# An explicit order for the attention stage, a wait for GpSimd's steps, twelve staged weight tiles and early fill matmuls

## The chip, the cores and the metric

The kernel runs on one core of one Trainium2 chip. The metric is the device time of one execution in microseconds (us). PE is TensorE, DVE VectorE, ACT ScalarE, POOL GpSimd, and SP the queue from which nearly all DMAs are issued. PE's clock has two levels here, 1.2 and 2.4 GHz; the profile gives the granted clock as a share of the higher one.

## What is computed

```python
# attention: q, k, v, a_re, a_im are (4, 8, 768, 48)
mag = np.sqrt(a_re * a_re + a_im * a_im)
scale = np.minimum(mag, 0.999) / (mag + 1e-06)
for t in range(S):
    S = (a_re * scale + i * a_im * scale)[t, :, None] * S + outer(k[t], v[t])   # complex S
    y[t] = q[t] @ real(S)
x = y.transpose(0, 2, 1, 3).reshape(3072, 384)
# first MLP: 8 experts, 384 -> 1024 -> 384, for tokens with x @ w_skip > 0
e_idx = argmax(x @ w_gate); gate = softmax(x @ w_gate)[e_idx]
x = x + gate * (relu(x @ w1[e_idx]) @ w2[e_idx])
# second MLP, all tokens: 384 -> 2048 -> 384
out = relu(x @ w_in) ** 2 @ w_out
```

## The kernel before

Three stages follow each other on the core: attention (to about 284 us), the first MLP, the second MLP.

Attention works on 12 units `u` (4 batches, 3 blocks of 256 positions), each with two chunks of 128 positions. For a unit, `load_a` brings a_re and a_im into two tiles of the pool `ws` (tags of 4 buffers each), `load_qk` brings q and k, `load_v` v. The front of a unit turns a into sums: `ln_r`, `inv_r`, `tangent`, `square`, `ln_s`, `ln_a`, `eps_a`, `fin_l` give the logarithm of the magnitude, `angle` the angle; `total_l` and `total_th` add two halves; `sum_l` and `sum_th` (L1000, L1008) sum them over positions with matmuls into the one PSUM buffer `cs`; `exp_l` and `exp_n` (ACT) give the scales, `whole_turns`, `rest_turns`, `abs_turns`, `cosine` and `sine` the rotations. Logarithm and exponential are one table of ACT, angle, sine and cosine another; going from one to the other issues a table load (L872). `scale_q`, `scale_k` (L1078, L1083), `rot_q`, `rot_k` (L1090, two instructions a unit each) and `shift` (L1105) apply them. For unit 0 the front is split into its two halves.

The core of attention runs over 48 half chunks `kk`: `turn_q`, `turn_k` (four transposes each, L1121), the copies `turned_q`, `turned_k` (L947 on DVE, L945 on ACT), `score` (L1142), `mask` (L1149, DVE), `from_state` (L1164) and `from_chunk` (L1173); and over 24 chunks `j`: `state` (L1184), `state_add`, `state_move`, `state_turn`, `state_turned`, `y_out`, `x_turn`, `x_out`, `x_store` (L1239), and the routing logits `logits`, `logits_out`, `logits_turn`, `logits_sum`. `route` (generators in small pieces) makes the lists of tokens for groups of chunks; after group 2, `gather_a` fetches the first 128 rows of expert 0, and `first_a`, `second_a` compute them at the end of attention.

Every one of these is a job with a queue (P, A, V, G, D for PE, ACT, DVE, POOL, SP), a cost, the jobs that it needs, and the buffers that it takes. `order()` runs a list scheduler over the jobs with due times from the tables `DUE`, `DUE_AT`, `START` and `PHASES`, and the jobs are emitted in the order found; each engine runs its own instructions in that order. `ENG` says which engine takes a copy or an elementwise step. `SHARED` names the steps of DVE that read or write SBUF only; the scheduler lets them and POOL's steps not overlap in its own model, but nothing in the program enforces it.

`load_w(i)` loads tile i of the first MLP's weights into the same pool `ws`. With `WS = 8`, tiles 0 to 7 (expert 0) are loaded in attention; tile 8 + 2g is issued after every second step of `first_rows` of the second half of expert 0's rows, and the second-matmul tiles 9, 11, 13, 15 after steps of `second_rows`. `split_w(i)` casts tile i on ACT (L2134) and takes the rest on DVE (L2135); `NEXT_SPLIT` places tiles 8, 10, 9 in the entry. In the main loop step s issues tile `s + WS`. Ahead of the first MLP `WARM` = 18 fill matmuls are issued (L2264).

## Time and profile before

| | us |
|---|---|
| median of 3 runs | 844.82 (844.55 to 845.34) |
| the profiled execution | 847.55 |
| its span, first to last instruction | 845.8 |
| PE, DVE, ACT, POOL busy | 809.1, 636.5, 402.3, 146.4 |

The profiled execution is 2.73 us longer than the median, and 1.75 us of its time lie outside its span. The busy time of PE is modelled from pipelined matmuls, so a stretch in which PE is shown as busy may still hold fewer matmuls than another; the number of matmuls in a stretch, the idle time before an instruction with its releaser, and the granted clock say more.

### The profile page before, as it was taken

How to read it: one execution, taken by the hardware profiler on the slowest of the kernel's cores; microseconds unless marked ns; L12 is line 12 of the kernel's file. 1: busy time of each engine (PE TensorE's matmuls, PEld its weight loads, DVE VectorE, ACT ScalarE, POOL GpSimd, SP SyncE). 2: the span in 40 equal slices, each digit the busy share in tenths (PEclk: the TensorE clock that was granted, in tenths of full speed). 3: DMA queues.
4: the chain of work that ended last, by engine and by line, in shares of the span. 5: the costliest groups of instructions: out<-in, count | busy, mean ns of one | idle time of the engine just before them, and what ended most of it. 6: DMA issues, size and time to landing. Idle time of an engine off the chain costs nothing.

```text
span 845.8 us, 14533 instructions
## 1 busy us (share of the span) xinstructions
PE 809.1 (96%) x5620; PEld 702.6 (83%) x5620; DVE 636.5 (75%) x1175; ACT 402.3 (48%) x691; POOL 146.4 (17%) x113
## 2 busy tenths in 40 slices
...
GB/s 181 175 181 96 161 122 138 122 103 108 151 146 109 165 297 273 241 241 242 106 107 93 94 112 1 38 0 162 98 83 133 136 175 149 159 141 76 1 1 41
DMA packets 177564, 109.01 MB, mean 129 GB/s; under 512 B 129811, under 2 KB 169001, under 8 KB 177488
## 3 DMA queue, kind: packets, MB, share of 16 engines
...
q0 software_dynamic: 2048, 5.45, 2.2%
q8 instruction: 46, 0.75, 0.4%
...
HBM read 91.52 MB, written 17.30 MB: 129 GB/s over the span
## 4 chain that ended last, share of the span: by engine, by line
PE 81%; DVE 10%; issue 3%; DMA 2%; POOL 1%; ACT 1%; SPq 1%; POOLq 0%; DVEq 0%; ACTq 0%
PE ph L2387 21%; PE po L2416 7%; PE po L2418 7%; PE po L2417 7%; PE ph L2162 7%; PE mp L1142 4%; PE pt L1121 4%; PE cs L1000 3%; PE yp L1173 2%; PE po L2182 2%; PE po L2183 2%; PE po L2184 2%; PE yp L1164 2%; PE up L1184 2%; PE xp L1230 1%
## 5 line engine op out<-in xcount | busy, mean ns | idle before, releaser
L2392 ACT ACTIVATE rl<-ph 128x512 f32<-128x512 f32 x96 | 57.4, 598 | 176.9 <-PE ph L2387 176.9
L2416 PE MATMUL po<-woh,gh 128*128 128x384 f32 x384 | 129.5, 337 | 1.1 <-DVE part L2423 1.1
L2418 PE MATMUL po<-woh,gl 128*128 128x384 f32 x384 | 129.6, 337 | 0.0
L2417 PE MATMUL po<-wol,gh 128*128 128x384 f32 x384 | 129.0, 336 | 0.0
L2394 DVE TENSOR_TENSOR gg<-rl,ph 128x512 f32<-128x512 f32 x96 | 65.9, 686 | 69.6 <-ACT rl L2392 69.6
L2387 PE MATMUL ph<-xh,wih 128*128 128x512 f32 x288 | 114.6, 398 | 0.0
L2387 PE MATMUL ph<-xh,wil 128*128 128x512 f32 x288 | 113.3, 393 | 0.0
L2399 DVE TENSOR_TENSOR gl<-gg,gh 128x512 fp32r<-128x512 f32 x96 | 66.3, 691 | 51.6 <-ACT gh L2397 34.4
L2397 ACT CAST gh<-gg 128x512 fp32r<-128x512 f32 x96 | 59.7, 622 | 88.7 <-DVE gg L2394 88.7
L2387 PE MATMUL ph<-xl,wih 128*128 128x512 f32 x288 | 81.9, 392 | 0.0
L2416 PEld LDWEIGHTS po<-woh,gh 128*128 128x128 f32 x384 | 72.2, 188 | 5.9 <-DVE part L2423 1.7
L2417 PEld LDWEIGHTS po<-wol,gh 128*128 128x128 f32 x384 | 72.1, 188 | 4.0
L2418 PEld LDWEIGHTS po<-woh,gl 128*128 128x128 f32 x384 | 72.0, 188 | 0.0
L2387 PEld LDWEIGHTS ph<-xl,wih 128*128 128x128 f32 x288 | 54.1, 188 | 12.4
L2387 PEld LDWEIGHTS ph<-xh,wih 128*128 128x128 f32 x288 | 53.9, 187 | 8.7 <-ACT xh L2377 0.2
L2387 PEld LDWEIGHTS ph<-xh,wil 128*128 128x128 f32 x288 | 54.2, 188 | 8.2
L1142 PE MATMUL mp<-qhT,khT 96*128 96x128 f32 x384 | 53.6, 285 | 1.4 <-ACT khT L945 1.2
L1090 POOL TENSOR_TENSOR kh<-kn,sc 128x768 f32<-128x768 f32 x22 | 46.1, 2109 | 39.9 <-ACT sc L876 37.6
L1142 PEld LDWEIGHTS mp<-qhT,khT 96*128 96x128 f32 x384 | 46.7, 193 | 6.6 <-issue 3.3
L2162 PE MATMUL ph<-xh,w1h 128*128 128x256 f32 x168 | 44.4, 293 | 2.5 <-DVE hl L2166 2.5
L2165 ACT ACTIVATE hh<-ph 128x256 fp32r<-128x256 f32 x56 | 21.4, 384 | 45.4 <-PE ph L2162 44.8
L2162 PE MATMUL ph<-xh,w1l 128*128 128x256 f32 x168 | 42.3, 280 | 0.0
...
## 6 DMA issues: line engine op xcount, KB each, us to landing
...
```

Of the source, the lines that this page charges most:

```text
L1090: eng("rot_" + n_, u).tensor_mul(x[n_ + "h"][:, c], x[n_ + "n"][:, c].unsqueeze(2).to_broadcast([128, H, 2, D]), scv)
L1121: nc.tensor.transpose(out=pt[0:96, i, :], in_=flat(u[nm], c, h), identity=ident)
L1142: nc.tensor.matmul(out=mp[:, i, :], lhsT=X[kk]["kh"][:, i, :], rhs=X[kk]["qh"][:, i, :], start=True, stop=True)
L2162: mm(out=ph, lhsT=w_[:, c0:c0 + 128], rhs=x_[:, kk], start=(i == 0), stop=(i == len(parts) - 1))
L2387: mm(out=ph, lhsT=w_[:, kk * 128:(kk + 1) * 128], rhs=x_[:, kk], start=(i == 0), stop=(i == len(parts) - 1),)
L2392: nc.scalar.activation(out=rl, in_=ph, func=AF.Relu)
L2394: nc.vector.tensor_mul(gg, rl, ph)
L2397: nc.scalar.copy(out=gh, in_=gg)
L2399: nc.vector.tensor_sub(gl, gg, gh.bitcast(FP32))
L2416: mm(out=po2[j][t], lhsT=a, rhs=wo[f][0], start=begin, stop=False)
L2417: mm(out=po2[j][t], lhsT=a, rhs=wo[f][1], start=False, stop=False)
L2418: mm(out=po2[j][t], lhsT=b_, rhs=wo[f][0], start=False, stop=end)
```

## The change

- The scheduler and its due tables go. `ORDER` is a written list of the 1262 jobs, and `order()` only asserts that each job stands behind what it needs. Which job stands where changes all over attention. In unit 0 the angles and their sums now stand ahead of the rest of the logarithm chain. `load_v` stands in the order of units.
- `ENG` gives many steps to another engine: of 48 each, DVE has 14 `khT` and 15 `qhT` copies (20 and 21 before); `rot_k` is on POOL for 5 units (11 before); `scale_q` and `scale_k` are on POOL for 8 and 6 units (5 and 2 before); `tangent` on POOL for 8 (6 before); `whole_turns` on DVE for 8 (3 before); `x_out` on DVE 6 times (10 before), `y_out` 8 times (12 before).
- The first instruction of each step of POOL (but `gather_a`) waits for the last instruction of the `SHARED` step of DVE that was emitted last before it.
- `WS` is 12: the pool has 6 buffers of each tag, tiles 0 to 11 are loaded in attention, and the later ones are issued at the old places with numbers 4 higher.
- `warm` issues 8 and 6 fill matmuls before attention's own begin, behind `inv_r` and `exp_n` of unit 0. `cst2` is loaded ahead of `cst`.
- `half_hi` and `half_lo` and the tables `HALVES_L`, `HALVES_TH` are added; both are empty, so that no such step is emitted. Costs in the jobs change and no longer have an effect.

```diff
--- before.py
+++ after.py
-DUE = {
...
-}
...
+ORDER = """
+load0.0 load0.1 ln_r.0.0 cst2 cst inv_r.0.0 clear tangent.0.0 square.0.0 ln_r.0.1 inv_r.0.1 tangent.0.1 ln_s.0.0 warm.0
+angle.0.0 square.0.1 angle.0.1 ln_a.0.0 eps_a.0.0 const load_a.1 sum_th.0.0 whole_turns.0.0 sum_th.0.1 rest_turns.0.0 more
+whole_turns.0.1 ln_s.0.1 ln_a.0.1 ln_r.1 fin_l.0.0 eps_a.0.1 inv_r.1 load0k.1 abs_turns.0.0 load_v.0 load0q.0 sum_l.0.0
+exp_n.0.0 exp_l.0.0 fin_l.0.1 rest_turns.0.1 tangent.1 abs_turns.0.1 sum_l.0.1 square.1 exp_n.0.1 scale_k.0.1 warm.1
+load0k.0 sine.0.0 from_state.0 scale_q.0.0 angle.1 scale_k.0.0 total_th.1 sum_th.1.0 cosine.0.0 rot_k.0.0 state.0 load_a.2
+sine.0.1 cosine.0.1 rot_k.0.1 load0q.1 ln_s.1 whole_turns.1.0 rest_turns.1.0 rot_q.0.0 ln_r.2 inv_r.2 load_a.3 turn_k.0
+turned_k.0 ln_a.1 eps_a.1 tangent.2 state_add.0 sum_th.1.1 turn_q.0 exp_l.0.1 turned_q.0 turn_q.1 turned_q.1 whole_turns.1.1
+rest_turns.1.1 turn_k.1 turned_k.1 scale_q.0.1 fin_l.1 total_l.1 score.0 score.1 turn_k.2 turned_k.2 mask.1 turn_k.3
+turned_k.3 abs_turns.1 square.2 ln_s.2 sum_l.1.0 from_state.1 ln_r.3 inv_r.3 load_qk.1 state.1 rot_q.0.1 turn_q.3 exp_n.1.0
...
+first_a.4 logits.23 logits_out.23 first_a.5 logits_turn.23 logits_sum.23 route.4.0 route.4.1 route.3.1000 second_a.0
+second_a.1 route.4.2 route.4.3 route.4.4 first_a.6 route.4.5 route.4.6 route.4.7 route.4.8 first_a.7 relu_a.1 second_a.2
+route.4.9 route.4.10 route.4.1000 second_a.3 second_a.4 x_turn.23 x_out.23 x_store.23 route_exp.4 second_a.5 x_store.22
+second_a.6 second_a.7 yo_a.0
+"""
...
+HALVES_L = ()
+HALVES_TH = ()
...
 ENG = {
-    "abs": "s", "abs@0": "v", "abs@1": "v", "abs@5": "v", "abs@6": "v", "khT": "s", "khT@3": "v", "khT@7": "v",
-    "khT@9": "v", "khT@10": "v", "khT@13": "v", "khT@14": "v", "khT@15": "v", "khT@17": "v", "khT@19": "v",
-    "khT@24": "v", "khT@28": "v", "khT@31": "v", "khT@32": "v", "khT@36": "v", "khT@37": "v", "khT@39": "v",
-    "khT@42": "v", "khT@44": "v", "khT@45": "v", "khT@47": "v", "ls": "s", "ls@0": "v", "ls@1": "v", "ls@2":
-    "v", "ls@4": "v", "ls@6": "v", "ls@7": "v", "ls@13": "v", "ls@15": "v", "ls@23": "v", "qhT": "s", "qhT@4":
-    "v", "qhT@7": "v", "qhT@9": "v", "qhT@10": "v", "qhT@11": "v", "qhT@12": "v", "qhT@14": "v", "qhT@15": "v",
-    "qhT@19": "v", "qhT@21": "v", "qhT@25": "v", "qhT@30": "v", "qhT@31": "v", "qhT@32": "v", "qhT@34": "v",
-    "qhT@35": "v", "qhT@36": "v", "qhT@42": "v", "qhT@43": "v", "qhT@44": "v", "qhT@45": "v", "rot_k": "g",
-    "rot_k@6": "v", "rot_q": "v", "rot_q@4": "g", "rot_q@9": "g", "rot_q@10": "g", "rot_q@11": "g", "scale_k":
-    "v", "scale_k@3": "g", "scale_k@4": "g", "scale_q": "v", "scale_q@0": "g", "scale_q@1": "g", "scale_q@5":
-    "g", "scale_q@6": "g", "scale_q@10": "g", "sd": "s", "sd@0": "v", "sd@1": "v", "sd@6": "v", "sd@7": "v",
-    "sd@10": "v", "sd@12": "v", "sd@14": "v", "sd@16": "v", "shift": "v", "shift@2": "g", "shift@5": "g",
-    "shift@11": "g", "sq": "v", "sq@0": "g", "sq@2": "s", "sq@4": "g", "sq@5": "g", "sq@6": "s", "sq@9": "s",
-    "sq@11": "s", "t": "v", "t@1": "g", "t@3": "g", "t@5": "g", "t@9": "g", "t@10": "g", "t@11": "g", "tot":
-    "g", "tot@1": "v", "tot@5": "v", "tot@7": "v", "whole": "s", "whole@0": "v", "whole@1": "v", "whole@4": "v",
-    "xn": "s", "xn@1": "v", "xn@4": "v", "xn@8": "v", "xn@11": "v", "xn@13": "v", "xn@14": "v", "xn@15": "v",
-    "xn@19": "v", "xn@20": "v", "xn@21": "v", "yT": "v", "yT@2": "s", "yT@3": "s", "yT@4": "s", "yT@7": "s",
-    "yT@8": "s", "yT@9": "s", "yT@12": "s", "yT@15": "s", "yT@18": "s", "yT@19": "s", "yT@20": "s", "yT@21": "s",
+    "abs": "s", "abs@0": "v", "abs@2": "v", "abs@6": "v", "abs@7": "v", "khT": "s", "khT@0": "v", "khT@2": "v",
+    "khT@3": "v", "khT@4": "v", "khT@6": "v", "khT@10": "v", "khT@12": "v", "khT@13": "v", "khT@14": "v",
+    "khT@15": "v", "khT@16": "v", "khT@21": "v", "khT@27": "v", "khT@44": "v", "ls": "s", "ls@3": "v", "ls@5":
+    "v", "ls@8": "v", "ls@13": "v", "ls@15": "v", "ls@17": "v", "ls@20": "v", "qhT": "s", "qhT@0": "v", "qhT@2":
+    "v", "qhT@7": "v", "qhT@10": "v", "qhT@13": "v", "qhT@23": "v", "qhT@26": "v", "qhT@28": "v", "qhT@29": "v",
+    "qhT@34": "v", "qhT@35": "v", "qhT@36": "v", "qhT@42": "v", "qhT@43": "v", "qhT@44": "v", "rot_k": "v",
+    "rot_k@4": "g", "rot_k@7": "g", "rot_k@9": "g", "rot_k@10": "g", "rot_k@11": "g", "rot_q": "v", "rot_q@0":
+    "g", "rot_q@1": "g", "rot_q@3": "g", "rot_q@11": "g", "scale_k": "v", "scale_k@2": "g", "scale_k@3": "g",
+    "scale_k@6": "g", "scale_k@9": "g", "scale_k@10": "g", "scale_k@11": "g", "scale_q": "g", "scale_q@0": "v",
+    "scale_q@5": "v", "scale_q@6": "v", "scale_q@8": "v", "sd": "s", "sd@0": "v", "sd@2": "v", "sd@6": "v",
+    "sd@13": "v", "sd@15": "v", "sd@16": "v", "sd@19": "v", "sd@21": "v", "shift": "v", "shift@4": "g",
+    "shift@7": "g", "shift@11": "g", "sq": "s", "sq@0": "v", "sq@1": "v", "sq@3": "v", "sq@5": "v", "sq@6": "v",
+    "sq@10": "g", "t": "g", "t@0": "v", "t@1": "v", "t@5": "v", "t@7": "v", "tot": "g", "tot@1": "v", "tot@2":
+    "v", "tot@11": "v", "whole": "v", "whole@4": "s", "whole@7": "s", "whole@8": "s", "whole@10": "s", "xn":
+    "s", "xn@0": "v", "xn@7": "v", "xn@8": "v", "xn@15": "v", "xn@18": "v", "xn@19": "v", "yT": "s", "yT@1":
+    "v", "yT@2": "v", "yT@5": "v", "yT@11": "v", "yT@13": "v", "yT@21": "v", "yT@22": "v", "yT@23": "v",
+    "half_hi": "s",
 }
...
 WARM = 18
+WARMS = (8, 6)
+WARM_AFTER = (("inv_r", 0, 0), ("exp_n", 0, 1))
 NEXT_SPLIT = {0: 8, 2: 10, 7: 9}
...
     def clear():
+        nc.gpsimd.memset(made["ones"], 1.0)
         nc.gpsimd.memset(made["ones_t"], 1.0 / TWO_PI)
-        nc.gpsimd.memset(made["ones"], 1.0)
         for t in vt:
             nc.gpsimd.memset(t, 0.0)
         nc.gpsimd.memset(wr, 0.0)
 
     def make_more():
         nc.gpsimd.memset(ones16, 1.0)
+        nc.gpsimd.tensor_copy(out=made["lo_r"], in_=C("lo"))
+        nc.gpsimd.tensor_copy(out=made["hi_r"], in_=made["hi"])
         nc.gpsimd.tensor_sub(strict16, C("lo"), ident)
         nc.gpsimd.tensor_copy(out=iota16, in_=C("iota"))
         nc.gpsimd.memset(run[:, 0, :], 0.0)
+
+    def warm(i):
+
+        if i == 0:
+            spare_bank[0] = ps_u.tile([128, 512], FP32, tag="u", name="warm")
+        for _ in range(WARMS[i]):
+            nc.tensor.matmul(
+                out=spare_bank[0][:, 0:128], lhsT=made["ones"], rhs=made["ones"], start=True, stop=True
+            )
 
...
-    WS = 8
+    WS = 12
...
         D_(("load0", 0), lambda: load0((("ar", a_re), ("ai", a_im)), 0), 2.2, takes=[("ar", fl_), ("ai", ft)])
+        D_(("cst",), lambda: load_const(True), 0.5)
         D_(("load0", 1), lambda: load0((("ar", a_re), ("ai", a_im)), 1), 2.2)
-        D_(("cst",), lambda: load_const(True), 0.5)
-        jobs["load_a", 1]["due"] = -1000 + next(n)
+        for i, after in enumerate(WARM_AFTER):
+            job(("warm", i), warm, (i,), "P", 0.222 * WARMS[i], [("clear",), after], [("u", [("warm", len(WARMS) - 1)])] if i == 0 else [])
         jobs["load_a", 1]["after"] = []
...
-        for key in (("load_v", 0), ("load_a", 2), ("load_qk", 1), ("load_v", 1)):
-            jobs[key]["due"] = -1000 + next(n)
         D_(("wr",), load_wr, 0.5, [("clear",)])
-        job(("clear",), clear, (), "G", 3.3, due=-1000)
-        job(("const",), make_const, (), "V", 0.9, [("cst",)], due=-5.0)
-        job(("more",), make_more, (), "G", 1.6, [("const",), ("cst2",)], due=0.0)
+        job(("clear",), clear, (), "G", 3.3)
+        job(("const",), make_const, (), "V", 0.9, [("cst",)])
+        job(("more",), make_more, (), "G", 2.4, [("const",), ("cst2",)])
         for i in range(WS):
-            job(("load_w", i), load_w, (i,), "D", 2.2, takes=[("ai" if i % 2 else "ar", [])], due=due("load_w", NU, 4, i) + 0.5 * i)
+            job(("load_w", i), load_w, (i,), "D", 2.2, takes=[("ai" if i % 2 else "ar", [])],
+                behind=[("load_w", i - 1) if i else ("load_a", NU - 1)])
         for i in range(3):
-            job(("load_raw", i), load_raw, (i,), "D", 4.4, due=due("load_raw", NU, 4, i) + 2 * i, after=[("load_w", WS - 1)])
+            job(("load_raw", i), load_raw, (i,), "D", 4.4, after=[("load_w", WS - 1)], behind=[("load_raw", i - 1)] * (i > 0))
 
     SIZE = dict(
-        ar=4, ai=4, qn=2, kn=2, r_=4, eL=2, eN=2, totl=1, totth=1, sc=2, qh=2, kh=2, tr_s=2,
...
+    def order():
+
+        by_name = {".".join(map(str, k_)): k_ for k_ in jobs}
+        out_ = [by_name[x] for x in ORDER.split()]
+        done, held = set(), {t: [] for t in SIZE}
+        for k_ in out_:
+            o = jobs[k_]
+            need = [*o["after"], *o["behind"]]
             for tag, r in o["takes"]:
...
+            assert done.issuperset(need), (k_, [x for x in need if x not in done])
+            done.add(k_)
+        assert len(out_) == len(done) == len(jobs)
         return out_
...
+    sync = mybir.DependencyInfo(mybir.DependencyClass.Sync, mybir.DependencyReason.DATA)
+    last_v = None
     for k_ in order():
-        jobs[k_]["f"](*jobs[k_]["args"])
+        o = jobs[k_]
+        n = len(nc.cur_bb.bb.instructions)
+        o["f"](*o["args"])
+        if o["shared"]:
+
+            e_ = nc.vector.engine if o["q"] == "V" else nc.gpsimd.engine
+            new = [i for i in nc.cur_bb.bb.instructions[n:] if i.engine == e_]
+            if o["q"] == "V":
+                last_v = new[-1]
+            elif last_v is not None:
+                tc.add_manual_dep(new[0], last_v.name, sync, reason="GpSimd's turn")
     attn.close()
 
     rout.close()
@@ -2122,7 +1796,6 @@
```

## Rows read from the trace of the kernel before

**Rows 1.** Page, first part: busy us, share of the span, instructions of each engine.
```profile
PE 809.1 (96%) x5620; PEld 702.6 (83%) x5620; DVE 636.5 (75%) x1175; ACT 402.3 (48%) x691; POOL 146.4 (17%) x113
```

**Rows 2.** Busy time by stretch: us, each engine's busy time, PE clock, DMA share, GB/s.
```profile
0.00:25.70 25.70, 9.22 (x20) 3.39 (x22) 12.61 (x22) 15.00 (x24) 13.32 (x24) 1.00 1.20 186
...
40.00:50.00 10.00, 8.27 (x79) 5.54 (x79) 9.30 (x12) 9.33 (x12) 6.87 (x4) 1.00 1.02 209
...
50.00:60.00 10.00, 8.79 (x69) 7.03 (x69) 8.71 (x17) 7.10 (x12) 3.32 (x3) 0.83 0.75 135
...
60.00:230.00 170.00, 168.92 (x1754) 128.94 (x1752) 150.96 (x306) 124.05 (x200) 69.24 (x42) 1.00 0.58 129
...
230.00:260.00 30.00, 26.79 (x288) 22.14 (x286) 26.32 (x48) 11.67 (x20) 14.21 (x10) 0.94 0.40 126
...
304.00:845.80 541.80, 532.26 (x2954) 491.73 (x2953) 387.49 (x663) 209.03 (x377) 27.32 (x25) 1.00 0.38 120
```

**Rows 3.** Timeline, 6 to 31 us: start, duration, engine, line, names, [idle before <-releaser].
```profile
6.64 0.52 ACT L876 ACTIVATE r__180<-ws 128x384 f32<-128x384 f32 x1
...
11.33 0.84 ACT L876 ACTIVATE r__203<-ws 128x768 f32<-128x768 f32 x1
...
15.90 1.28 ACT L872 ACT_TABLE_LOAD   x1
...
17.19 0.52 ACT L876 ACTIVATE ws<-ws 128x384 f32<-128x384 f32 x1
...
17.77 1.65 PE L1000 MATMUL cs<-ws,hi_t 128*128 128x384 f32 x2 [2.80 <-ACT ws L876]
...
23.07 4.50 POOL L1090 TENSOR_TENSOR kh<-kn,sc 128x768 f32<-128x768 f32 x2 [3.95 <-ACT sc L876]
...
25.77 1.22 PE L1184 MATMUL up<-kh,vt 128*64 128x96 f32 x16
...
30.82 1.05 PE L1142 MATMUL mp<-qhT,khT 96*128 96x128 f32 x8
```

**Rows 4.** Timeline, 45 to 49 us.
```profile
45.98 4.33 POOL L1090 TENSOR_TENSOR kh<-kn,sc 128x768 f32<-128x768 f32 x2 [0.40 <-ACT sc L876]
...
45.99 2.63 DVE L1090 TENSOR_TENSOR qh<-qn,sc 128x768 f32<-128x768 f32 x1 [0.57 <-POOL tot L989]
...
48.67 0.64 PE L1121 MATMUL pt<-cst,qh 128*96 128x128 f32 x4 [1.48 <-DVE qh L1090]
```

**Rows 5.** Timeline, 242 to 251 us.
```profile
242.71 1.75 DVE L1402 TENSOR_TENSOR run<-run,fill 128x8 bf16<-128x8 bf16 x1
...
246.27 1.75 DVE L1409 SCALAR_TENSOR_TENSOR spot<-part_l,idx_a 128x1 f32<-128x1 f32 x1
...
250.23 0.43 PE L1246 MATMUL lp<-yT,wr 128*32 128x128 f32 x8 [1.61 <-DVE xn L947]
...
250.82 1.64 PE L1142 MATMUL mp<-qhT,khT 96*128 96x128 f32 x8 [0.17 <-DVE qhT L947]
```

**Rows 6.** One line (ns min/median/max); groups by line, 0 to 300 us; POOL's waits.
```profile
L1090 DVE TENSOR_TENSOR qh<-qn,sc x16: 948/952/2627, 24.6 to 193.2; 128x768 f32<-128x768 f32 x16
...
L947 DVE COPY qhT<-pt 96x512 f32<-96x512 f32 x21 | 14.3, 680 | 1.5 <-PE pt L1121 1.3
...
L1090 POOL TENSOR_TENSOR kh<-kn,sc 128x768 f32<-128x768 f32 x22 | 46.1, 2109 | 39.9 <-ACT sc L876 37.6 <-issue 2.3
...
L872 ACT ACT_TABLE_LOAD x15 | 19.2, 1283 | 1.0 <-PEq L2552 0.7
...
POOL kh L1090 <- ACT sc L876: 37.6, 8, 8.4
```

**Rows 7.** Timeline, 294 to 304 us.
```profile
294.58 4.90 SPq L835 DMA_DIRECT2D ws<-in_moe_w_dram  x4
...
300.98 0.83 ACT L2134 CAST w2h<-ws 128x768 fp32r<-128x768 f32 x1 [2.79 <-DMA ws<-in_moe_w_dram]
...
303.71 0.39 PE L2162 MATMUL ph<-xh,w1h 128*128 128x256 f32 x1 [2.50 <-DVE hl L2166]
```

More of the change, by code (lines that the diff above doesn't have):

```diff
@@ new lines @@
+score.2 exp_l.1.1 tangent.3 fin_l.2 total_l.2 square.3 exp_n.1.1 score.3 sine.1 state_turn.0 mask.2 mask.3 y_out.0 sum_l.2.0
+x_turn.0 state_turned.0 wr from_state.2 from_chunk.2 scale_q.1 from_state.3 from_chunk.3 cosine.1 scale_k.1 angle.3
+rot_k.1.0 rot_k.1.1 state.2 load_a.4 angle.2 shift.1 state_move.1 total_th.2 state_add.2 exp_l.2.0 exp_n.2.0 load_a.5
+turn_k.5 turned_k.5 turn_k.7 turned_k.7 rot_q.1.0 sum_l.2.1 exp_n.2.1 load_qk.2 turn_k.4 turned_k.4 turn_k.6 y_out.1 x_out.0
+exp_l.2.1 x_store.0 ln_s.3 state_turn.1 state_turned.1 sum_th.2.0 turned_k.6 rot_q.1.1 ln_r.4 inv_r.4 state.3 turn_q.4
@@ new lines @@
+from_chunk.11 y_out.5 exp_l.4.1 inv_r.7 turn_k.13 turned_k.13 logits_turn.4 logits_sum.4 sum_th.4.1 total_l.5 from_state.12
+tangent.7 state.6 state_add.6 ln_s.6 turn_k.12 whole_turns.4.1 rest_turns.4.1 x_turn.4 state_turn.6 square.7 ln_s.7
+rot_q.3.1 x_out.4 sum_l.5.0 exp_l.5.0 logits.5 turned_k.12 ln_a.6 state_turned.6 total_th.5 exp_n.5.0 abs_turns.4
+logits_out.5 turn_k.15 eps_a.6 score.12 ln_a.7 logits_turn.5 logits_sum.5 turned_k.15 mask.12 route.0.0 route.0.1 route.0.2
+sum_l.5.1 exp_n.5.1 exp_l.5.1 from_state.13 x_store.4 turn_k.14 load_v.4 route.0.3 cosine.4 score.13 sine.4 fin_l.6
@@ new lines @@
+ln_r.8 inv_r.8 tangent.8 turn_k.21 turned_k.21 sum_th.6.0 whole_turns.6.0 rest_turns.6.0 logits_turn.9 score.20 mask.20
+state_turn.9 state_turned.9 square.9 logits_sum.9 sum_th.6.1 whole_turns.6.1 rest_turns.6.1 abs_turns.6 total_th.7 score.21
+turn_q.23 x_turn.9 square.8 state_turn.10 turned_q.23 scale_q.6 mask.21 ln_s.8 scale_k.6 cosine.6 sine.6 rot_k.6.0 turn_k.22
+turn_q.22 turned_q.22 score.23 load_qk.7 x_store.8 turned_k.22 sum_th.7.0 whole_turns.7.0 rot_q.6.0 from_state.20
+state_turned.10 from_state.21 from_chunk.20 rest_turns.7.0 from_chunk.21 rot_q.6.1 x_out.9 x_store.9 angle.8 y_out.10
```

419 lines of the change are left out of this document (166 added, 253 removed), and 297 rows, old and new, of the table DUE_AT.

## The prediction

> **What bounds the kernel now.** I read the page first, then busy time by stretch, then PE's waits in time order at the places where a stretch falls behind. PE is busy 96% of an 845.8 us span, DVE 75%, POOL 17% [rows 1], so an edit pays only where PE stands idle or runs at half clock. By stretches [rows 2], everything from 304 us on (two MLP stages, 541.8 us) and the middle of attention (60 to 230 us, 168.92 of 170 us busy, clock 1.00) leave little: the middle issues 1754 matmuls in 170 us, 10.3 a us. Five places lag: the start, where the first state matmul comes at 25.77 us and the first score at 30.82 [rows 3]; 40 to 60 us; 230 to 260 us; and the entry of the first MLP, 284 to 304 us.
>
> **The start** is a chain over ACT, DVE and POOL [rows 3]. ACT finishes the whole log/exp chain of unit 0 and only then loads the trigonometric table (15.90, 1.28 us); the first angle is at 17.19, the first sum of angles at 17.77 (after 2.80 us of idle PE), and the first rotation is two POOL instructions from 23.07, 2.25 us each.
>
> The change takes unit 0's angles first. Worked with the same rows' durations, ACT: ln and exp of both halves end at 7.16 as now (6.64 + 0.52); ln_s 7.68; table 1.28, 8.96; angle 0.52, 9.48. The squares it needs go from POOL to DVE. cst is now issued behind cst2 (204 KB, 1.1 us at the 186 GB/s of this stretch [rows 2]); DVE reaches the steps that read it at about 8.9, after tangents, squares and ln_a, so this is hidden unless cst lands over 1 us later still. The sum of angles starts at 9.9 instead of 17.77. Then the log chain is the long one: second angle 10.0, table 11.3; eps_a and ln_s at 0.52, ln_r of unit 1 at 0.84, eps_a, inv_r of unit 1, 14.5; three exponentials from PSUM, as wide as a half, 16.1; table 17.4; sine, angle of unit 1, cosine, 19.3. rot_k.0.0 is now on DVE, 0.95 us [rows 6] and some 0.15 of hand-over: ready at 20.4. So the first state moves from 25.77 to about 21. The first score has sum_th.1.0, state.0, turn_k.0, sum_th.1.1 (which needs the one cs buffer back from DVE, at 23.2) and three turns ahead: 25.6 instead of 30.82. Before that point the old kernel had one more state done (0.8 us). **Gain 4.4 us.** Bounds 2 and 5.5: q and the first half of k of unit 0 are moved behind load_a.1, the second half of k and v; with them 2.77 MB stand in the queue, 15 us at 186 GB/s, so k lands at 16 or 17 us, ahead of its scaling at 18.3; 4 us late and the gain is 2. load_a.3 now stands ahead of load_qk.1 on SP's queue; qk of unit 1 is scaled only after score.3, so that is covered by over 5 us. The 14 fill matmuls (some 3 us at full clock) lie in 5 to 9 and 16 to 20 us, where PE has nothing: cost 0 while those gaps are there, up to 1.5 us if the second lot runs at half clock into sum_th.1.0. They may shorten the first sums (two took 1.65 us at 17.77); I take none of it.
>
> **40 to 60 us** [rows 2, 4]: PE idles 1.73 and 1.21 us, and in 50 to 60 the granted clock is 0.83, which is 17% of 10 us or 1.7 us more. Excess 4.6 us. The cause is seen at 45.99: a DVE rotation takes 2.63 us, where the median is 952 ns [rows 6], while POOL begins its own at 45.98. PE waits 1.48 us for it at 48.67. The new order spreads these steps, and a POOL step may no longer start ahead of the DVE step listed before it. I take half, **2.3 us**, bounds 0 and 4.6, because the chain ACT-DVE-PE of units 1 to 3 remains: ACT gets four more table switches (19 by the list, 15 now [rows 6]), 4 x 1.28 = 5.1 us over attention, two of them before 40 us.
>
> By the Trainium skill, ScalarE: Activation LUTs, "What ACT_TABLE_LOAD costs", a switch is about 1.28 us of load plus 1.38 us of drain, 2.66 us in all; by that the four would cost 10.6 us of ACT, an estimate from that page. Here the load takes 1.28 and the next ACT step starts 0.01 us behind it (15.90 + 1.28, then 17.19) [rows 3], so no drain is seen behind it.
>
> **Moved work, whole attention** (counted in the two engine tables, priced by [rows 6]). Off DVE: 12 turned copies and 4 y copies at 0.68, 4 x copies and 2 small ones at less, some 13.5 us; 7 units of scales and 2 tangents at 0.95, 8.6. Onto DVE: 12 rotations at 0.95, 11.4; 10 whole_turns at 0.68, 6.8. Net DVE about -4 us. POOL loses 12 rotations at 2.1 (25 us) and gains scales and tangents at up to that price: about -9. ACT takes the copies, gives up the whole_turns and pays 5.1 for its tables: about +12. No engine becomes the bound: DVE has about 151 of 170 us in the middle [rows 2], ACT 124. In the middle PE is dense already, so I take **0.5 us**, bounds -8 (a wait of 0.45 us for each of the 18 POOL rotations) and +4.
>
> **230 to 260 us** [rows 2, 5]: 3.2 us idle, clock 0.94, with a score of 8 matmuls at 1.64 us at 250.82 against 1.05 at 30.82 [rows 3]; 6% of 30 us is 1.8 more, 5.0 together. Two DVE steps on 8 and 1 elements take 1.75 us each, at 242.71 and 246.27, each beside a POOL rotation, and DVE's copy of x, for which PE then waits 1.61 us before 250.23, stands behind them. The list puts group 2's last routing steps ahead of POOL's late rotations, and those must wait. **2.5 us**, half, bounds 0 and 5.0.
>
> By the Trainium skill, SBUF — State Buffer, "Who interferes with whom", whichever of the two engines starts first holds the shared pair for its whole instruction. The two rows of 1.75 us agree. It speaks against the change too: the added wait holds back POOL only, and a DVE step listed behind a POOL step blocks as before. That is the first rival.
>
> **Entry of the first MLP** [rows 7]. The tile for step 8's second matmul (tile 9) is issued at 294.58, with a queue of four; ACT's cast waits 2.79 us for it and starts at 300.98; the relu behind it on ACT is late, and PE idles 2.50 us before 303.71. With 12 tiles, tile 9 is loaded in attention, where the DMA engines are 40% busy from 230 to 260 us [rows 2]. What is late next: tile 13 is issued where 9 was, lands at about 300.9 and is cast after step 10's relu, some 302: margin about 1 us. **Gain 2.5 us**, bounds 1.2 (13 late) and 2.9. Four more 384 KB loads stand on SP's queue among x stores and ahead of load_raw; a load delays the store behind it by its issue, under half a us, and only the gather waits for stores. Two extra POOL copies at the start and the unused half_hi code cost nothing on the path: POOL idles there.
>
> **Sum.** 4.4 + 2.3 + 0.5 + 2.5 + 2.5 = 12.2. The profiled execution took 847.55, so 835.35 on its own scale; the runs' median is 844.82, 2.73 below, so **832.6 us**. The forecast's own range, with the two halved terms and the start each about 2 us to either side, is 827 to 838.
>
> **Rivals.**
> 1. *The port stall stays*: DVE still stands behind POOL's instructions, and only start and MLP entry pay: 4.4 + 2.5 = 6.9, 837.9 us. For it: POOL keeps over 50 instructions of some 2 us. Against: POOL loses about 9 us of them. Chance 0.20.
> 2. *The list pays everywhere*: all upper bounds, 5.5 + 4.6 + 4 + 5.0 + 2.9 = 22.0, 822.8 us. For it: each excess has a visible cause. Against: dense PE in the middle. 0.10.
> 3. *POOL's wait reaches PE* (slower): a rotation on POOL that now waits a DVE step (0.95) although its sine is ready. PE takes rotations directly; 18 of them at 0.95 cost 17.1 us against 12.2: +4.9, 849.7 us. It decides from 0.68 us a rotation. For it: POOL stood ready and waited 37.6 us in 8 waits for ACT's sine or cosine ahead of kh [rows 6], so a second wait can become the last. Against: no matmul waits long for POOL now, and POOL has most of its time free. 0.14.
> 4. *The change doesn't do what it says*: the in-order queues drift apart from the list, and new PE waits in the middle (up to the 8 us bound) eat what the start and the entry give, 6.9 us: about 844.8 us. 0.09.
>
> The forecast has 0.47. Range 822.5 to 844: it leaves out rival 3 and the ends of rivals 2 and 4. Of rival 4, 0.06 is within 0.2% (1.7 us, about what a measurement of this kernel can tell from no change), 0.02 faster and 0.01 slower. Faster 0.47 + 0.20 + 0.10 + 0.02 = 0.79, same 0.06, slower 0.14 + 0.01 = 0.15.
>
> **What would show it.** Right: first score near 25.6 us, first angle sum near 10, no tiny DVE step of over 1 us in the stretch before the gather, no wait of ACT for a weight tile at the entry, first first-MLP step some 10 us earlier, and the time from there to the end shorter by 2.5 only. Wrong: PE waits on POOL's rotations in the middle; fewer than 10 matmuls a us there; k or q of unit 0 landing after 19 us; PE waiting for tile 13.

## The result and the profile after

The kernel after takes 825.5 us (median of 4 runs, 823.5 to 827.2), against 845.1 us for the kernel before on the same chip (844.6 to 846.7): a ratio of 0.976, with a 95% interval of 0.974 to 0.979. The medians thus differ by 19.6 us. The profiled execution took 824.69 us with a span of 822.9, which is 22.9 us below the span of before: of the two profiled executions, that of before was on the slow side of its runs. The prediction, 832.6 us, had the sign, and its range of 822.5 to 844 us holds the time; the forecast's own range, 827 to 838, does not. Its sum of 12.2 us is 7.4 us short of the medians and 10.7 us short of the two spans.

First PE, PEld (PE's weight loads), DVE, ACT and POOL over the whole span, from the page of after (busy us, share of the span, instructions), to be held against [rows 1]:

```profile
PE 794.9 (97%) x5648; PEld 706.9 (86%) x5648; DVE 614.0 (75%) x1168; ACT 411.4 (50%) x709; POOL 128.7 (16%) x108
```

The shares hardly move; PE is 97% busy instead of 96%. The stretches say more. Busy time by stretch of after, with the columns of [rows 2] (length; PE, PEld, DVE, ACT and POOL with their instructions; PE's clock; DMA share; GB/s):

```profile
0.00:25.70 25.70, 16.66 (x76) 11.40 (x76) 16.21 (x31) 20.06 (x29) 7.32 (x21) 0.80 1.25 183
40.00:50.00 10.00, 9.86 (x102) 7.54 (x100) 9.91 (x21) 9.21 (x17) 5.29 (x3) 1.00 0.93 192
50.00:60.00 10.00, 10.00 (x98) 7.41 (x94) 9.93 (x17) 9.91 (x17) 3.88 (x4) 1.00 1.10 207
60.00:230.00 170.00, 167.31 (x1919) 140.06 (x1920) 147.47 (x322) 133.95 (x222) 72.53 (x48) 1.00 0.67 148
230.00:260.00 30.00, 27.92 (x282) 23.39 (x278) 18.07 (x70) 7.06 (x15) 1.38 (x2) 1.00 0.37 122
```

Read the counts, not the busy time. From 60 to 230 us PE is shown busy for 167.31 us, less than the 168.92 of before, and yet issues 1919 matmuls instead of 1754: 11.3 a us instead of 10.3. From 40 to 60 us it issues 200 instead of 148.

The start, PE of after in order of time (start, duration, engine, line, operation, [idle before <- releaser]):

```profile
9.34 1.65 PE L833 MATMUL cs<-ws,hi_t 128*128 128x384 f32 x2 [4.56 <-ACT ws L686]
...
19.93 0.91 PE L833 MATMUL cs<-ws,hi_t 128*128 128x384 f32 x2 [0.86 <-ACT ws L686]
...
21.63 0.88 PE L1017 MATMUL up<-kh,vt 128*64 128x96 f32 x16 [0.47 <-DVE kh L923]
...
26.67 1.99 PE L975 MATMUL mp<-qhT,khT 96*128 96x128 f32 x16
```

The first sum of angles comes at 9.34 instead of 17.77, the first state at 21.63 instead of 25.77, the first score at 26.67 instead of 30.82 [rows 3].

The end of attention, again PE of after. Rows of before that answer to them follow, since they are not among those shown above:

```profile
253.42 0.60 PE L1063 MATMUL xp<-cst,yT 128*128 128x128 f32 x4
...
255.79 2.13 PE L1937 MATMUL idle<-iota,ones 128*128 128x256 bf16 x18
262.00 0.88 PE L1941 MATMUL px<-cst,gx 128*128 128x128 f32 x3 [4.08 <-DMA gx<-xb,idx_g]
...
263.58 2.93 PE L1314 MATMUL ph<-xh,ws 128*128 128x128 f32 x12 [0.70 <-ACT xh L1943]
```

```profile
283.90 2.13 PE L2264 MATMUL idle<-iota,ones 128*128 128x256 bf16 x18
285.86 0.49 PE L2268 MATMUL px<-cst,gx 128*128 128x128 f32 x3
287.05 1.60 PE L1481 MATMUL ph<-xh,ws 128*128 128x128 f32 x12 [0.70 <-ACT xh L2270]
```

Attention ends (where the fill matmuls ahead of the first MLP begin) at 255.79 us instead of 283.90, 28.1 us earlier. Part of that is given back at once: PE now waits 4.08 us for a gather that was hidden before, and the 12 matmuls behind the wait take 2.93 us instead of 1.60. The granted clock of 262 to 267 us is 0.50, the lower level; in before it is 1.00 from 285 to 290 us.

The first matmul of the first MLP's main loop, in after and then in before:

```profile
277.14 0.57 PE L1835 MATMUL ph<-xh,w1h 128*128 128x256 f32 x1
```

```profile
298.62 0.57 PE L2162 MATMUL ph<-xh,w1h 128*128 128x256 f32 x1
```

Three times of each profiled run divide the difference: the end of attention, the entry (from there to that first matmul), and the rest of the span. This table covers the experiments below too; "against after" is the difference of the two ratios times 845.1 us, negative where faster.

| kernel | median us | ratio to before (95%) | against after, us | attention ends | entry | rest |
|---|---|---|---|---|---|---|
| before | 845.1 | 1 | +19.9 | 283.9 | 14.7 | 547.2 |
| after | 825.5 | 0.976 (0.974 to 0.979) | 0 | 255.8 | 21.4 | 545.8 |
| nowait | 853.6 | 1.008 (1.006 to 1.010) | +26.5 | 287.3 | 20.9 | 544.7 |
| old_wait | 840.2 | 0.992 (0.990 to 0.994) | +13.4 | 277.8 | 14.7 | 547.6 |
| old_engines | 878.9 | 1.039 (1.037 to 1.041) | +53.2 | 309.5 | 20.9 | 545.1 |
| old_list | 854.4 | 1.010 (1.008 to 1.012) | +28.3 | 292.6 | 14.7 | 545.1 |
| tail | 818.1 | 0.968 (0.965 to 0.970) | -7.5 | 258.6 | 14.7 | 544.8 |
| fill54 | 821.8 | 0.974 (0.971 to 0.976) | -2.2 | 256.1 | 18.8 | 545.0 |
| early8 | 825.1 | 0.976 (0.974 to 0.978) | -0.1 | 258.6 | 22.0 | 544.5 |
| nofill | 824.9 | 0.976 (0.974 to 0.978) | -0.5 | 260.8 | 20.5 | 544.8 |
| turn | 822.8 | 0.972 (0.970 to 0.974) | -3.6 | 254.4 | 21.6 | 545.6 |
| tail_turn | 816.7 | 0.965 (0.963 to 0.967) | -9.5 | 253.6 | 15.4 | 545.3 |
| tail_early8 | 819.8 | 0.970 (0.968 to 0.972) | -5.6 | 257.3 | 15.4 | 545.0 |
| both_ways | 827.3 | 0.977 (0.975 to 0.980) | +0.8 | 258.5 | 21.4 | 545.6 |

So the 22.9 us of the two spans are 28.1 (attention) - 6.6 (entry) + 1.4 (rest). Kernels with the list of after differ by up to 5 us in the end of attention from one profiled run to the next: PE's wait for the first gather was 1.69 us in after and 2.45 and 2.68 us in early8 and nofill, and in these two the granted clock of 210 to 230 us was 0.91 and 0.83, where it was 1.00 in after. A difference of that size in this column alone says nothing.

### The profile page after: what moved, and what is told of

It reads as the page before. It is cut to its first block, busy times and chain, and to the rows that moved or that the text cites. A ratio compares the mean times of both kernels' runs of the same rounds, so it can differ in the third digit from the quotient of the medians.

```text
span 822.9 us, 14590 instructions
## 1 busy us (share of the span) xinstructions
PE 794.9 (97%) x5648; PEld 706.9 (86%) x5648; DVE 614.0 (75%) x1168; ACT 411.4 (50%) x709; POOL 128.7 (16%) x108
## 4 chain that ended last, share of the span: by engine, by line
PE 84%; DVE 8%; ACT 3%; DMA 2%; issue 1%; POOL 1%; SPq 0%; DVEq 0%; POOLq 0%; ACTq 0%
PE ph L2060 22%; PE po L2089 7%; PE po L2091 7%; PE po L2090 7%; PE ph L1835 7%; PE pt L954 5%; PE mp L975 4%; PE cs L833 3%; PE po L1855 2%; PE po L1856 2%; PE po L1857 2%; PE yp L1006 2%; PE yp L997 2%; PE po L1320 1%; PE xp L1063 1%
## 5 line engine op out<-in xcount | busy, mean ns | idle before, releaser
L975 PE MATMUL mp<-qhT,khT 96*128 96x128 f32 x384 | 50.3, 277 | 0.0
L1855 PE MATMUL po<-w2h,hh 128*128 128x384 f32 x112 | 37.8, 338 | 0.0
```

The lines of the kernel that those rows point to most:

```text
L975: nc.tensor.matmul(out=mp[:, i, :], lhsT=X[kk]["kh"][:, i, :], rhs=X[kk]["qh"][:, i, :], start=True, stop=True)
L1855: mm(out=o_, lhsT=p, rhs=a_, start=(f == 0), stop=False)
```

## The experiments

**The wait taken out of after (nowait).**

```diff
-            elif last_v is not None:
-                tc.add_manual_dep(new[0], last_v.name, sync, reason="GpSimd's turn")
```

> The kernel after, with the list and engines as they are, but GpSimd's steps no longer wait for the VectorE step ahead. Theory 1 (the wait buys part of the gain: without it a POOL step starts beside a DVE step and stretches it to over 1.5 us, as in rows 4 and 5): about 829 us, 3 to 6 us slower than after, with DVE steps of 1.7 to 2.6 us back in the trace. Theory 2 (the order alone brings the gain, the wait only fixes what the list already has): 825 us, within 1 us of after. Rival (the wait holds POOL up for more than it saves): 822 us or less.

Measured: 853.6 us, 26.5 us slower than after and slower than the kernel before. Both theories and the rival were far too low; theory 1 had the mechanism, DVE steps stretched beside POOL steps. The worst place, first DVE, then POOL, then PE of nowait, in order of time:

```profile
232.00 1.61 DVE L1246 TENSOR_TENSOR gate_a<-part_l 128x1 f32<-128x1 f32 x1
...
235.00 0.65 DVE L881 SCALAR_TENSOR_TENSOR sc<-sc,cs 128x480 f32<-128x480 f32 x1
235.57 5.55 DVE L923 TENSOR_TENSOR qh<-qn,sc 128x768 f32<-128x768 f32 x1
...
231.78 1.82 POOL L923 TENSOR_TENSOR kh<-kn,sc 128x768 f32<-128x768 f32 x1 [11.71 <-DMA qn<-in_q_dram]
...
234.96 1.84 POOL L923 TENSOR_TENSOR kh<-kn,sc 128x768 f32<-128x768 f32 x1
236.74 1.81 POOL L911 TENSOR_TENSOR qn<-qn,eL 128x768 f32<-128x768 f32 x1
238.50 1.80 POOL L916 TENSOR_TENSOR kn<-kn,eN 128x768 f32<-128x768 f32 x1
...
241.18 1.94 PE L954 MATMUL pt<-cst,qh 128*96 128x128 f32 x8 [5.05 <-DVE qh L923]
```

DVE's rotation begins 0.61 us behind a POOL step, and POOL has two more steps ready. The rotation ends at 241.12, 0.82 us behind the last of the three (238.50 + 1.80 = 240.30): it is held for all of them, 5.55 us instead of 0.95. PE waits 5.05 us for it and then runs 8 transposes in 1.94 us, which take 1.08 us at 24.77 in after. At 232.00 a step on one element of each partition takes 1.61 us beside another POOL step. The same two steps in after:

```profile
207.22 0.15 DVE L1246 TENSOR_TENSOR gate_a<-part_l 128x1 f32<-128x1 f32 x1
...
209.33 1.05 DVE L923 TENSOR_TENSOR qh<-qn,sc 128x768 f32<-128x768 f32 x1
...
207.73 1.84 POOL L923 TENSOR_TENSOR kh<-kn,sc 128x768 f32<-128x768 f32 x1 [1.36 <-DVE gate_a L1247]
...
211.45 1.84 POOL L923 TENSOR_TENSOR kh<-kn,sc 128x768 f32<-128x768 f32 x1
```

To size it over attention, sum over DVE's steps of the first 300 us what each takes beyond the usual time of its tile and shape (the lower quartile over the runs), where that is over 0.15 us. This gives some 33 us in nowait, 23 in before, 14 in old_wait, 4.5 in after and nothing in both_ways. (Taken with the usual time of each run alone, before comes to 18; the order stays the same.) The 28 us between nowait and after stand beside the 31.5 us by which attention ends later (287.3 against 255.8). That the missing wait costs the 26.5 us is shown by the run. That it does so through the held steps is shown where PE waits behind one, 5.05 us here; for the rest it is argued from the two sums. That POOL has hold of something which DVE needs (the prediction's port) is read from the overlap in the rows.

**The wait alone, put into before (old_wait).** Its planner, order, engines and 8 tiles stay.

```diff
     for k_ in order():
-        jobs[k_]["f"](*jobs[k_]["args"])
+        o = jobs[k_]
+        n = len(nc.cur_bb.bb.instructions)
+        o["f"](*o["args"])
+        if o["shared"]:
...
+            elif last_v is not None:
+                tc.add_manual_dep(new[0], last_v.name, sync, reason="GpSimd's turn")
```

> The kernel before, with nothing but the wait added: its planner, order, engines and 8 early tiles stay. Theory 1 (the wait by itself is worth the port stalls of 40 to 60 and 230 to 260 us): about 840 us, 4 to 5 us faster than before. Theory 2 (in an order that was not made for it the wait moves the delay from DVE to POOL, whose rotation of 2 us then starts later): 845 to 849 us, no gain or a loss.

Measured: 840.2 us, ratio 0.992, 6.5 us faster than before (5.0 to 8.1 by the interval); theory 1 holds, with a little more than its 4 to 5 us. Busy time of old_wait by stretch:

```profile
40.00:50.00 10.00, 9.04 (x88) 6.45 (x86) 8.92 (x13) 9.33 (x14) 4.65 (x3) 1.00 1.02 209
50.00:60.00 10.00, 8.36 (x69) 6.33 (x70) 9.26 (x16) 8.60 (x14) 4.25 (x3) 0.89 0.86 153
60.00:230.00 170.00, 170.00 (x1763) 130.03 (x1763) 149.03 (x308) 123.96 (x199) 64.29 (x42) 1.00 0.58 130
230.00:260.00 30.00, 29.86 (x346) 25.09 (x342) 24.06 (x55) 13.87 (x24) 14.20 (x10) 1.00 0.47 153
```

The gain lies in 230 to 260 us, where PE's idle time falls from 3.21 to 0.14 us and the clock rises from 0.94 to 1.00 [rows 2]. The middle stays at 1763 matmuls (1754), although DVE's held time falls from some 23 to 14 us over attention. So in the old order the wait only repairs the place where the kernel had stalled visibly.

**The new list with the old engines (old_engines), the old order with the new engines (old_list).** The first replaces only the table `ENG`; the second replaces `ORDER` by the order that the planner of before finds, with tiles 8 to 11 behind tile 7 and no early fill (and the assertion on the list no longer asks for the order of the loads). Both keep the wait. Of the first edit, the first line of each side:

```diff
 ENG = {
-    "abs": "s", "abs@0": "v", "abs@2": "v", "abs@6": "v", "abs@7": "v", "khT": "s", "khT@0": "v", "khT@2": "v",
...
+    "abs": "s", "abs@0": "v", "abs@1": "v", "abs@5": "v", "abs@6": "v", "khT": "s", "khT@3": "v", "khT@7": "v",
...
```

> The kernel after with the list as it is, but the table that gives the copies and elementwise steps to engines is that of before. Theory 1 (the order carries the gain of the middle): about 829 us, up to 5 us slower than after, the matmul count of 60 to 230 us stays over 1860. Theory 2 (the choice of engines carries it, with the order only following): 838 us or more, the count falls towards the 1754 of before.

> The kernel after with the order of the kernel before as its list (tiles 8 to 11 right behind tile 7, no early fill matmuls), but with the new table of engines, the wait and 12 early tiles. Theory 1 (the order carries the gain): 840 to 845 us, not more than the 2.5 us of the tile faster than before, plus or minus 3. Theory 2 (engines and wait carry it): 832 us or less. The entry of the first MLP has no 2.5 us wait for a weight tile in either.

Measured: 878.9 and 854.4 us. In old_list both theories fall. In old_engines theory 1 falls; theory 2 has the side (838 or more), but the count falls far below the 1754 of before, and the kernel is 33 us slower than before, which neither theory had. So neither half carries the gain alone. The middle of old_engines, then of old_list:

```profile
60.00:230.00 170.00, 142.69 (x1483) 113.17 (x1481) 136.22 (x261) 112.07 (x176) 49.94 (x33) 0.97 0.49 103
```

```profile
60.00:230.00 170.00, 161.14 (x1641) 121.36 (x1641) 132.85 (x263) 124.75 (x204) 56.41 (x37) 0.99 0.54 117
```

PE idles 27 and 9 us of the middle. Why each half is slower alone is not shown by one run. Two things are seen: DVE's held time, summed as above, is some 25 us in old_engines and 14 in old_list although both have the wait, so with another order or other engines DVE steps again start behind POOL's; and in old_engines PE waits 8.5 us for rotations on POOL (4.1 + 2.3 + 2.1), which no matmul of after does. The rest is argued: a list fixes the order on five queues, and a copy that goes to another engine then stands behind work that the list had not put ahead of it. Either way list, engines and wait are one schedule here.

**The last chunk of x earlier (tail).** The list is wrapped anew in the kernel; only the names around each move are shown, here and in turn.

```diff
-x_store.21 route.3.20
+x_store.21 x_store.22 route.3.20
...
-logits.23 logits_out.23
+logits.23 x_turn.23 x_out.23 x_store.23 logits_out.23
...
-second_a.4 x_turn.23 x_out.23 x_store.23 route_exp.4 second_a.5 x_store.22 second_a.6
+second_a.4 route_exp.4 second_a.5 second_a.6
```

> The kernel after with one move at the end of the list: the turn, copy and store of the last chunk of x stand right behind logits.23, ahead of the second matmuls of the early rows, and the store of chunk 22 right behind that of chunk 21. Theory 1 (the 4.1 us wait of PE at 262 us is the gather, issued 5.9 us behind its list of indices because these stores are issued last): the gather is issued about 4 us earlier, the wait goes and with it the half clock of the first matmuls behind it: 820 us, 4 to 6 us faster than after. Rival (the gather is held by its own issue on POOL or by what stands ahead of it there, not by the stores): 825 us, the same wait.

Measured: 818.1 us, 7.5 us faster than after, 1.5 more than the upper end of what was expected. The reason for the wait in after, SP's queue, then DVE and POOL:

```profile
254.56 0.32 SPq L1072 DMA_DIRECT2D xb<-xn  x1
...
255.40 0.46 SPq L1072 DMA_DIRECT2D xb<-xn  x1
...
252.47 0.17 DVE L1285 SCALAR_TENSOR_TENSOR idx_g<-part_l 128x16 int32<-128x16 f32 x1
...
258.32 1.07 POOL L1790 DMA_INDIRECT gx<-xb,idx_g  x1 [30.73 <-DVE g_end L1186]
```

The indices are there at 252.64, but POOL issues the gather at 258.32. The rows of x that it reads are stored last: x_turn.23 stands behind second_a.4 on PE (253.42 above), and the last two stores into xb are issued at 254.56 and 255.40. The profile names another step, DVE's g_end, as what ended POOL's idle time; it ends at 258.05 (257.89 + 0.16), just ahead of the gather, and would be a rival. The run tail rules it out: there g_end runs at 260.66, 4.5 us behind the issue of the gather. In tail, on SP, DVE, POOL and PE:

```profile
251.34 0.32 SPq L1075 DMA_DIRECT2D xb<-xn  x1
...
255.67 0.18 DVE L1288 SCALAR_TENSOR_TENSOR idx_g<-part_l 128x16 int32<-128x16 f32 x1
...
256.12 0.99 POOL L1793 DMA_INDIRECT gx<-xb,idx_g  x1 [27.91 <-DVE idx_g L1288]
...
258.55 2.13 PE L1940 MATMUL idle<-iota,ones 128*128 128x256 bf16 x18
260.52 0.49 PE L1944 MATMUL px<-cst,gx 128*128 128x128 f32 x3
261.71 1.60 PE L1317 MATMUL ph<-xh,ws 128*128 128x128 f32 x12 [0.70 <-ACT xh L1946]
```

With the last store 4.8 us ahead, the gather follows its indices (ready at 255.85 in this run) by 0.27 us instead of 5.68. It is issued 2.4 us ahead of the end of attention and not 2.5 behind it, PE does not wait for it, and the entry is 14.7 us, that of before.

**More fill matmuls (fill54).**

```diff
-WARM = 18
+WARM = 54
```

> The kernel after with 54 instead of 18 fill matmuls ahead of the first MLP, so that PE does not idle while it waits for the gather. Theory 1 (the wait costs twice: 4.1 us of idle PE and, since the granted clock falls in it, about 2 us more in the 20 matmul groups behind it): about 823.5 us, 1.5 to 2.5 us faster than after, the first MLP's first matmuls at 1.6 instead of 2.9 us a group. Rival (the fill matmuls outlast the gather, or the clock falls anyway): 825 to 827 us.

Measured: 821.8 us, 2.2 us faster than after, the size that theory 1 gave; the intervals of the two ratios overlap, so the trace decides. PE of fill54, then the stretch of 262 to 267 us (columns as above) in after and in fill54:

```profile
256.06 6.06 PE L1937 MATMUL idle<-iota,ones 128*128 128x256 bf16 x54
262.11 0.52 PE L1941 MATMUL px<-cst,gx 128*128 128x128 f32 x3
263.33 1.60 PE L1314 MATMUL ph<-xh,ws 128*128 128x128 f32 x12 [0.70 <-ACT xh L1943]
```

```profile
262.00:267.00 5.00, 4.30 (x19) 3.90 (x20) 0.01 (x1) 0.86 (x2) 2.95 (x3) 0.50 0.55 156
```

```profile
262.00:267.00 5.00, 4.30 (x37) 3.98 (x36) 0.28 (x1) 1.55 (x4) 3.16 (x4) 1.00 0.59 183
```

px starts at the same time as in after (262.11 and 262.00), but the matmuls behind it run at a granted clock of 1.00 instead of 0.50: 1.60 us for 12 instead of 2.93, and 37 matmuls in the 5 us instead of 19, with PE shown as busy for 4.30 us in both. The entry is 2.5 us shorter. Thus of the 6.6 us that the entry lost, 2.5 are clock and some 4 are the wait.

**Twelve buffers, but only eight tiles loaded early (early8, tail_early8).**

```diff
+    EARLY = 8
...
-        for i in range(WS):
+        for i in range(EARLY):
...
-            load_w(WS + 2 * g)
+            load_w(EARLY + 2 * g)
...
-            load_w(WS + f)
+            load_w(EARLY + f)
...
-        if s + WS < NS:
-            load_w(s + WS)
+        if s + EARLY < NS:
+            load_w(s + EARLY)
```

> The kernel after with the pool of 12 weight buffers, but only tiles 0 to 7 loaded in attention; tiles 8 and later are issued at the places of before. Theory 1 (the early tiles are worth the wait for tile 8 in rows 7): the cast on ACT waits again for its DMA, and the time is 827.5 to 828 us, 2 to 3 us slower than after. Rival (at the entry the wait for the gather, 4.1 us, covers the tile): 825 to 826 us, within 1 us of after.

> The move of the last chunk of x, but again only tiles 0 to 7 loaded in attention. Theory 1 (the 2.5 us of the early tiles were hidden behind the wait for the gather, and count once that wait is gone): 820 to 821 us, 2 to 3 us slower than with the move alone (818.05 us), and a wait of ACT for a tile's DMA that PE feels at the entry. Rival (the tile is not late any more, since the later loads start earlier too): 818 us, no such wait.

Measured: early8 825.1 us, the same as after. With the gather out of the way, tail_early8 takes 819.8 us against 818.1 for tail, with intervals that overlap widely, so that its time alone decides nothing between theory 1 (820 to 821) and the rival (818). Its profile does: it has no wait of ACT for a tile, the entry is 15.4 us (as in tail_turn, which has the early tiles) and the rest 545.0. Theory 1 falls in both. What held the tile in before is seen in SP's waits of before from 272 to 303 us (who waited for whom: us, times, longest):

```profile
SPq L840 <- PE ph L1481: 12.9, 1, 12.9
```

SP waits there until PE has read a buffer, and issues tile 8's load at 288.69, 4.8 us behind the end of attention. With 12 buffers SP does not wait for a buffer there and issues it as soon as it reaches it, in early8 0.7 us behind the end of attention and in tail_early8 6.3 us ahead of it:

```profile
259.28 0.40 SPq L654 DMA_DIRECT2D ws<-in_moe_w_dram  x1
```

```profile
250.96 0.40 SPq L654 DMA_DIRECT2D ws<-in_moe_w_dram  x1
```

The buffers give the gain, not the place in the list.

**No fill matmuls at the start (nofill).**

```diff
-WARM_AFTER = (("inv_r", 0, 0), ("exp_n", 0, 1))
+WARM_AFTER = ()
```

The jobs `warm.0` and `warm.1` also leave the list.

> The kernel after without the 14 fill matmuls of the first 20 us. Theory 1 (they only fill idle PE; the granted clock of 0 to 25.7 us is 0.80 with them): 825 us, within 0.7 us of after. Rival (without them the first sums of angles, turns and scores run at half clock): 826.5 to 828 us, and the granted clock of the first 26 us falls below 0.70.

Measured: 824.9 us, not to be told from after. The trace shows what the fill does, PE of nofill:

```profile
19.97 1.65 PE L836 MATMUL cs<-ws,hi_t 128*128 128x384 f32 x2 [3.15 <-ACT ws L689]
...
27.93 1.99 PE L978 MATMUL mp<-qhT,khT 96*128 96x128 f32 x16
```

After the 12 fill matmuls of after the same sum takes 0.91 us (19.93 above). The first score comes at 27.93 instead of 26.67, so the fill is worth 1.3 us there; the spread of the runs (822.3 to 828.0) hides it. By the time theory 1 holds; what the rival named, a first sum at half speed, is there too, but only 1.3 us of it reaches the first score. The rival's sign is not: the granted clock of 0 to 25.7 us is 1.00 in nofill, although the sum takes 1.65 us, and 0.80 in after. In this stretch that column does not tell how fast the matmuls ran.

**The early rows' turn later (turn), both moves (tail_turn).**

```diff
-logits_sum.19 turn_a.0 turn_k.40
+logits_sum.19 turn_k.40
...
-mask.40 score.42 x_turn.19
+mask.40 score.42 turn_a.0 x_turn.19
```

> The kernel after with one job moved: PE's turn of the early gathered rows (turn_a.0) stands behind score.42 instead of behind logits_sum.19, some 3 us of other matmuls later. Theory 1 (the wait for this gather, 1.7 us in the run of after and 2.4 to 2.7 us with a falling clock in three runs since, is on PE's path): 822 to 823.5 us, 2 to 3.5 us faster than after, no wait for this gather left. Rival (what is gained comes back in the wait for the last gather at the entry, 4.1 us, which lands when its stores have landed): 825 us, that wait longer by as much.

> Both moves together: the last chunk of x early (as in the run with that move alone, 818.05 us) and the turn of the early rows later. Theory 1 (two separate waits): 814 to 816 us, 2 to 4 us faster than with the first move alone. Rival (attention's end then comes before the last gather lands, and the wait at the entry returns): 817 to 818 us.

Measured: 822.8 and 816.7 us. PE had waited 1.69 us for the first gather in after (2.44 in tail); in both new runs that wait is gone. In turn the wait for the last gather stays at 3.94 us, so the rival's longer wait is not there, and the time is 3.6 us below after, by intervals that just touch: theory 1, a little above its 2 to 3.5 us. tail_turn, the fastest kernel measured here, is 9.5 us faster than after and 2.0 faster than tail by the ratios (0.965 and 0.968, intervals that overlap). Its 816.7 us lie between theory 1 (814 to 816) and the rival (817 to 818); the trace has no wait for a gather at the entry, so the rival's mechanism is out, and the gain over tail is not shown beyond the noise.

**The wait in both directions (both_ways).**

```diff
-    last_v = None
+    last_v = last_g = None
...
             if o["q"] == "V":
+                if last_g is not None:
+                    tc.add_manual_dep(new[0], last_g.name, sync, reason="VectorE's turn")
                 last_v = new[-1]
...
+                last_g = new[-1]
```

> The kernel after, with the wait in the other direction as well: a VectorE step on SBUF waits for the GpSimd step listed last ahead of it. Theory 1 (a DVE step that starts beside a running POOL step is held until that one ends, so waiting ahead of it costs no more): 825 us, within 2 us of after, the 4.1 us of stretched DVE steps turned into idle time ahead of them. Rival (such steps share the port and do some of their work beside POOL's, so that a full wait costs time): 830 us or more.

Measured: 827.3 us, 0.8 us above after by the ratios and not to be told from it; theory 1. The longest of DVE's waits for POOL in both_ways, 0 to 260 us:

```profile
DVE st L1036 <- POOL kh L923: 1.7, 2, 1.5
```

In after:

```profile
211.78 1.94 DVE L1036 TENSOR_TENSOR st<-st,tr 128x384 f32<-128x384 f32 x1
```

This step is stretched beside POOL's rotation from 211.45 (above); in both_ways it waits up to 1.5 us and then runs at its usual 0.55. No stretched step is left, and nothing is won. DVE's waits for POOL are 11.3 us in all here against 2.5 in after, more than the 4.5 us of stretched steps that went; no change of the time beyond the noise comes of either.

## Why the prediction was right or wrong

- **Start: right, a little less.** The first score comes 4.15 us earlier (30.82 to 26.67), where the prediction had 5.2; it took 0.8 off for a state matmul that the old kernel had done by then, which leaves 3.3 measured against its 4.4, inside its bounds. The first angle sum came at 9.34 (9.9), the first state at 21.63 (about 21), the first score at 26.67 (25.6). The fill matmuls, put at cost 0 and gain 0, give 1.3 us of this.
- **40 to 60 us, middle and 230 to 260 us: mis-sized, 5.3 us against 24.** Attention is 28.1 us shorter, of which 4.15 are the start. The step that failed is "in the middle PE is dense already", worth 0.5 us. I read 168.92 of 170 us busy [rows 2] as no room, although I had put the count of 1754 matmuls beside it. At the rate of after, 11.3 a us, the 1754 matmuls take 155.4 us, 14.6 less than 170. That is an estimate and a high one, since matmuls differ in length: with each kind weighed by its median interval over four of the runs it comes to about 9. So 5 to 9% of the stretch was time in which PE is shown as busy and did not advance; that this was many small waits is my reading, no run singles them out. From 40 to 60 us the 148 matmuls take 14.8 us at the 200 of after, 5.2 less, where I had halved the excess to 2.3. The Trainium skill, Perfetto Trace Analysis, opening note, says that matmul busy time is a bad measure of how close a kernel is to its limit, because matmuls are pipelined. The trace agrees: less busy time in after, 167.31 us, and more matmuls. A row that I had did show room: PEld, PE's weight loads, busy for 128.94 of the 170 us [rows 2], and for 140.06 in after.
- **The port stall: mechanism right, size wrong.** I priced it where PE visibly idled: two places, 4.8 us. The wait alone in the old order gave 6.5, close to that, and nearly all of it at 230 to 260 us; the half that I expected at 40 to 60 us came only with the new order. What I missed is that the new list depends on the wait: without it the change would have been 6.6 us slower than before (nowait, ratio 1.008). By my terms taking it out should have cost 4.8 us; it cost 26.5. So the wait is not a term to be added to the list's: in the new order it is worth four times what it is worth in the old one.
- **First rival, a DVE step behind a POOL step blocks as before.** It does (1.94 us at 211.78 in after), but only 4.5 us of it are left, and both_ways shows that a full wait wins nothing there. By the Trainium skill, SBUF — State Buffer, "Who interferes with whom", a DVE instruction with two SBUF inputs contends with GpSimd and one with a single SBUF input outside the two-port modes does not; in nowait the step at 235.00, which reads PSUM and SBUF, takes its usual 0.65 us beside a POOL step, the one at 235.57 with two SBUF inputs is held. The trace agrees.
- **Third rival, POOL's wait reaches PE: no.** No matmul of after waits for a rotation on POOL; the largest wait of DVE for POOL is 2.1 us. What the rival describes is seen in old_engines, where PE waits 8.5 us for rotations on POOL.
- **Entry: the tile right, the gather missed.** No wait of ACT for a tile is left and the rest of the span is 1.4 us shorter in after, 1.6 to 2.7 in the other runs with 12 buffers and the new entry (2.5 predicted, 1.2 at the low end). The cause was the number of buffers rather than the early loads. The failed step is "only the gather waits for stores": I wrote that and did not follow where the list puts the last two stores, behind the second matmuls of the early rows. That cost 6.6 us. The two errors have opposite signs: the gain was put 24 - 5.3 = 18.7 us too low in attention and 6.6 us too high at the entry, so with the smaller misses at the start and behind the entry the total was only 10.7 us short of the 22.9. That the range holds is in part luck: without the second error the time is that of tail, 818.1 us, and lies below the range.
- **Second rival, the list pays everywhere (822.8 us), was the nearest number**, but for its own reason only in part: the middle gave more than its upper bound of 4, and the entry took 6.6 us back. I gave it a chance of 0.10 because of the dense middle, the same misreading.

What stays open: how much of the middle belongs to single moves of the list, and by what single waits. Order, engines and wait could not be taken apart, since the wait alone gives 6.5 us and the order or the engines without the other are slower than before.
